# Batch 0's v loaded by key block for six heads, and the first transposes of batch 1 one column block sooner

## The chip, the cores and the metric

The kernel runs on one core of one Trainium2 chip. The metric is the device time of one launch in microseconds (us), the median of several runs. One further execution was taken with the hardware profiler; all times of single instructions below are from it, counted from its first instruction.

The engines have short names in the profile: PE is TensorE (matrix products and transposes), DVE is VectorE, ACT is ScalarE, POOL is GpSimd, SP is SyncE. Each runs its own list of instructions in order and waits on semaphores for the others. Loads and stores (DMAs) are issued by SP, ACT or POOL and then run by themselves.

## The reference

A decayed causal attention over 8 batches of 8 heads, followed by a two-layer network with an exact GELU. Cut to what is computed:

```python
# q, k, v: (8, 8, 576, 64)   f: (8, 8, 576)   w_in: (512, 2048)   w_out: (2048, 512)
scores = q @ k.T / sqrt(64)
cum    = cumsum(log(clip(f, 1e-4, 1)))
scores = where(causal, scores + cum[i] - cum[j], -1e9)
attn   = softmax(scores)
x      = (attn @ v).transpose(0, 2, 1, 3).reshape(8 * 576, 512)
out    = gelu(x @ w_in) @ w_out
```

## The kernel before

**Stages.** Each batch has an attention stage, four pairs of heads at a time, and then gemm1 (x @ w_in with GELU) by column blocks of 128 of the 2048 hidden columns. gemm2 (g @ w_out) of a batch is spread into the attention of the next one. The order on every engine is the order in which the program issues it; nothing is reordered by a scheduler. Batch 0 has its own `first_attention`, batch 1 its own `second_attention`, batches 2 to 7 share `attention`. The last 64 rows of all batches go through one more gemm1 and gemm2 at the end.

**v and the decay.** The decay is folded into v: `weigh_v(b, i)` (L288) multiplies v of pair i with a weight per key into the bf16 tile `vw`, with one more column that gives the softmax's denominator. The tile `v_sb` has the shape [128 keys, 8 heads, 5 key blocks, 64]. For batch 0 blocks 0 to 3 are filled by a loop over the heads on POOL's queue (L168 to L172), one load of 128 KB per head; block 4 has a load of its own later (`load_v` with block 4, L134). The helper `load_v(b, h0, h1, eng, ns)` loads v by key block instead: one load per block n for the heads h0 to h1.

**Where v of batch 0 is used.** In `first_attention` DVE does `weigh_v` of pairs 0 and 1, POOL that of pairs 2 and 3. Ahead of the latter POOL issues block 0 of w_in, block 4 of v and block 1 of w_in (`load_w_in` L184). The POOL queue has at most eight loads under way: a load waits for the landing of the eighth before it.

**The chain of batch 0's attention.** `scores_0` (L619) writes the scores of 128 keys against a range of queries, with the causal mask added by PE; ACT takes the exponential (L624). `attend_0(i, h)` (L650) multiplies the exponentials with `vw` into a PSUM bank `o`; the pool `o_psum` has two banks, in turn. `divide` (L663 reciprocal, L664 product) reads the bank, so that attend_0(1, 0) waits for the division of (0, 0), and so on. `to_xT_0` (L674) transposes the result on PE, and a copy (L677) puts it where gemm1 reads it.

**q and k.** In batches 0 and 1 they are transposed on PE: `transposes_first(b, i, ...)` (L226) makes 36 transposes of 64x64 for pair i into two banks of `o_psum`, and DVE copies them to `qT[i]` and `kT[i]` (L241). The q and k rows of heads 0 to 3 of batch 1 come with two loads that POOL issues in `first_attention`.

**gemm1 of batch 0.** `gemm1(c, ffb)` (L405) takes four matmuls of 128x512 for column block ffb and then a gelu on ACT (L425). Column blocks 0 to 3 are in `first_attention`, 4 to 9 in the loop at the end of the kernel, and 10 to 15 are held back for `second_attention`. The loop hangs other work behind some column blocks:

```python
                if ffb == 7:
                    weigh_v(1, 0)
                    load_w_out(0)
                    weigh_v(1, 1)
                    load_w_out(1)
                    load_qk_tokens(2)
                if ffb == 8:
                    transposes_first(1, 0, o_psum, "o")
```

`second_attention` begins with a switch of ACT's table to the exponential (L894) and with `scores` (L319) of pair 0, two tiles; then come the transposes of pair 1, two held column blocks and the next two tiles of scores. The scores' pool `s_psum` has two buffers, and ACT's exponentials (L329) free them.

Of the kernel before, what the change touches and what calls it, by code (L numbers as in the profile page):

```python
# [18 lines left out]
H = 8  # L19
HP = 4  # L20
NBLK = 5
# [33 lines left out]
def kernel(  # L55
# [10 lines left out]
    nc = tc.nc  # L66
# [31 lines left out]
    def load_qk_tokens(b, h0=0, h1=H):  # L98

        if b >= B:  # L100
            return
        stacked = b < 2
        if b not in qk_of:
            qk_of[b] = [
                qk_pool.tile(
                    [P, H // 2, J0 * D] if stacked else [PT, H, JT * D],
                    BF16,
                    tag=n,
                    name=f"{n}{b}",
                )  # L110
                for n in "qk"
            ]
        for which, src in enumerate((q, k)):
            if stacked:
                half, g0 = divmod(h0, H // 2)
                g1 = h1 - half * (H // 2)
                dst = qk_of[b][half][which * D : (which + 1) * D, g0:g1, :]
            else:
                dst = qk_of[b][which][:, h0:h1, :]
            nc.gpsimd.dma_start(  # L120
                dst,
                src[b, h0:h1].rearrange(
                    "h (p j) d -> p h (j d)", j=J0 if stacked else JT
                ),
            )
# [3 lines left out]
    def load_v(b, h0=0, h1=H, eng=nc.sync, ns=range(NBLK)):  # L129
        if b >= B:  # L130
            return
        for n in ns:
            p0 = D if n == NBLK - 1 else 0
            eng.dma_start(  # L134
                v_sb[p0:P, h0:h1, n, :],
                v[b, h0:h1, K0[n] + p0 : K0[n] + P].rearrange("h p d -> p h d"),
            )
# [27 lines left out]
    load_qk_tokens(0, 4, 6)  # L165
    diagonal(after, Alu.is_ge, -1.0e9, D)
    load_qk_tokens(0, 6, 8)
    for h in range(H):  # L168
        nc.gpsimd.dma_start(
            v_sb[:, h, 0 : NBLK - 1, :],  # L170
            v[0, h, 0:TC].rearrange("(n p) d -> p n d", p=P),
        )  # L172

    qT = [consts.tile([P, S], BF16, name=f"qT{i}") for i in range(HP)]
    kT = [consts.tile([P, S], BF16, name=f"kT{i}") for i in range(HP)]
# [10 lines left out]
    def load_w_out(c):  # L186
        kt = slice(c * n_ff // 4, (c + 1) * n_ff // 4)
        nc.gpsimd.dma_start(w_out_sb[:, kt, :], w_out_r[:, kt, :])
# [94 lines left out]
    def weigh_v(b, i, eng=nc.gpsimd, n0=0, n1=NBLK):  # L283

        hs = slice(2 * i, 2 * i + 2)
        bh = b * H + 2 * i
        w = wT[:, n0:n1, bh : bh + 2].rearrange("p n h -> p h n")
        eng.tensor_tensor(  # L288
            vw(b)[:, hs, n0:n1, 0:D],
            v_sb[:, hs, n0:n1, :],  # L290
            w.unsqueeze(3).to_broadcast([P, 2, n1 - n0, D]),
            Alu.mult,
        )
        if b:
            eng.tensor_copy(vw(b)[:, hs, :, D], w)
# [104 lines left out]
    def gemm1(c, ffb, kts=range(4), ps=None, act=True):  # L400
        src = xT(c) if c < B else tails
        if ps is None:
            ps = m_psum.tile([P, TC], FP32, tag="m", name="ps1")
        for kt in kts:
            nc.tensor.matmul(  # L405
                ps,
                w_in_sb[:, kt, ffb * P : (ffb + 1) * P],
                src[:, kt, 0:TC],
                start=(kt == 0),
                stop=(kt == n_dm - 1),  # L410
            )
        if n_dm - 1 in kts and act:
            gelu(c, ffb, ps)
        return ps

    def spare():
        return o_psum.tile([P, TC], FP32, tag="o", name="ps1")

    def gelu(c, ffb, ps):
        if c not in g_of:  # L420
            g_of[c] = [
                g_pool.tile([P, TC], BF16, tag=f"g{n}", name=f"g{n}")
                for n in range(n_ff)
            ]
        nc.scalar.activation(g_of[c][ffb], ps, Act.Gelu)  # L425
# [253 lines left out]
    def attend_tail():  # L679
        o = o_psum.tile([P, NBLK, D + 1], FP32, tag="o", name="o")  # L680
        for i in range(HP):
            for n in range(NBLK):
                e, c = e0_of[i, n, True]
                for h in range(2):
                    nc.tensor.matmul(
                        o[h * D : (h + 1) * D, i, :],
                        e[:, h, c + TC : c + S],
                        vw_of[0][:, 2 * i + h, n, :],
                        start=(n == 0),
                        stop=(n == NBLK - 1),  # L690
                    )
        x = x_pool.tile([P, NBLK, 2, D], BF16, tag="x", name="x")
        x_of[0, "tail"] = x.rearrange("p n h d -> p (n h) d")[:, 0:HP]
        divide(x_of[0, "tail"], o, HP)

    def tail_0():
        ps = o_psum.tile([P, HP, TL], BF16, tag="o", name="ps_x")
        for i in range(HP):
            for h in range(2):
                d = slice(h * D, (h + 1) * D)  # L700
                nc.tensor.transpose(
                    ps[d, i, :], x_of[0, "tail"][d, i, :], ident_bf[d, d]
                )
        nc.vector.tensor_copy(tails[:, :, 0:TL], ps)
# [176 lines left out]
    def second_attention():  # L881


        b, fill = 1, gemm2_first(0)

        def av(i, h):
            attend(b, i, h, (0, 1, 2, 3, 4))
            normalize(b, i, h)

        def transposes(i, pool, tag):  # L890
            transposes_first(b, i, pool, tag)


        nc.scalar.activation(warm[0:1, 0:1], warm[0:1, 0:1], Act.Exp)  # L894
        def tiles(i, t):
            scores(b, i, t)
            scores(b, i, t + 1)

        def run(i):
            av(i, 0)  # L900
            av(i, 1)

        tiles(0, 0)
        transposes(1, o_psum, "o")
        gemm1_hold(10)
        gemm1_hold(11)
        tiles(0, 2)
        gemm1_hold(12, nc.scalar.copy)
        transposes(2, o_psum, "o")
        tiles(1, 0)  # L910
        gemm1_hold(13)
        run(0)
        tiles(1, 2)
        gemm1_hold(14, nc.scalar.copy)
        transposes(3, o_psum, "o")
        weigh_v(1, 2)
        tiles(2, 0)
        gemm1_hold(15)
        run(1)
        weigh_v(1, 3)  # L920
        tiles(2, 2)
        take(fill, 4)
        tiles(3, 0)
        transpose_dma(2, 0, 4)
        transpose_dma(2, 4, 8)
        to_xT(b, 0, nc.vector.tensor_copy, o_psum, "o")
        to_xT(b, 1, nc.vector.tensor_copy, o_psum, "o")
        take(fill, 4)
        tiles(3, 2)
        behind(qk_of[2][1], H - 1)  # L930
        load_w_out(2)
        load_w_out(3)
        run(2)
        take(fill, 4)
        av(3, 0)
        take(fill, 4)
        both = s_psum.tile([P, 2, 1024], BF16, tag="s", name="ps_x2")
        to_xT(b, 2, nc.scalar.copy, ps=both[:, 0, 0:XC])
        av(3, 1)
        gemm1_begin(1, both)  # L940
        x_tail(1)
        load_v(2)

    for b in range(B):
        if b == 0:
            first_attention()
        elif b == 1:
            second_attention()
        else:
            attention(b)  # L950
        for ffb in range(4 if b < 2 else 5, n_ff):
            if b == 0 and ffb in HELD:
                continue
            aside = ffb in (7, 8) if b > 1 else b == 1 and ffb % 4 < 2
            gemm1(b, ffb, ps=spare() if aside else None)
            if b == 1 and ffb % 2 == 0:
                at = HELD[(ffb - 4) // 2]
                gelu(0, at, h_of[at])
            if b == 0:
                if ffb == 4:  # L960
                    attend_tail()
                if ffb == 5:
                    tail_0()
# [3 lines that stand above are left out]
                    weigh_v(1, 1)  # L967
                    load_w_out(1)
                    load_qk_tokens(2)
                if ffb == 8:  # L970
                    transposes_first(1, 0, o_psum, "o")
            elif b + 1 < B:
                first, gap = (5, 3) if b == 1 else (1, 4)
                at, late = divmod(ffb - first, gap)
                if late == 0:
                    untangle(b + 1, at)
                if late == gap - 2 and (b > 1 or at < 2):
                    weigh_v(b + 1, at)
                if ffb == (9 if b == 1 else 14):
                    load_qk_tokens(b + 2)  # L980
# [34 lines left out]
```

## Time and profile before

| | |
|---|---|
| three runs | 336.19, 333.74, 334.04 us |
| median | 334.04 us |
| the profiled execution | 335.58 us |
| its span, first to last instruction | 333.8 us |
| PE busy | 325.1 us (97%) |
| ACT, DVE, POOL busy | 205.5, 184.2, 134.2 us |
| PE's granted clock | 1.000 |

Busy times are sums over the span; the engines overlap. A DMA's landing is the time at which its data have arrived. A line such as `13.68 1.08 issue` of the chain has the start, the length, and the engine with its line; "issue" is time in which the engine waited for nothing that the profile shows. In a timeline a row has start, length, engine, line, operation, what is written from what, the count, and in brackets the idle time before it and what ended that.

### The profile page before, as it was taken

What the parts mean: (1) busy time and instruction counts of PE and PEld (TensorE: products, weight loads), DVE (VectorE), ACT (ScalarE), POOL (GpSimd) and SP (SyncE); (2) the same over time, 40 slices, a digit from 0 to 9 for tenths busy, and PEclk for the clock granted to TensorE, in tenths of its full rate; (3) what the DMA queues carried; (4) which work ended last, traced back from release to release, by engine and by line L of the source; (5) the groups of instructions that cost most, each with busy time, mean ns of one, the idle gap of its engine ahead of it and who ended that gap; (6) DMA issues with size and microseconds to landing.
All of it is one profiled execution on the core that took longest, in us unless ns stands there. A gap on an engine that the chain in (4) does not pass through costs nothing.

```text
span 333.8 us, 8055 instructions
## 1 busy us (share of the span) xinstructions
PE 325.1 (97%) x3287; PEld 170.1 (51%) x3287; DVE 184.2 (55%) x427; ACT 205.5 (62%) x296; POOL 134.2 (40%) x260
## 2 busy tenths in 40 slices
PE   8899999999999999999999999999999999999995
PEld 4664555445554466445644565455544654444443
DVE  5852657474549855894589547954795450010011
ACT  4786886974535786478736892788278836405600
POOL 8897873039327054704472354534442420000000
PEclk9999999999999999999999999999999999999999
DMA  7899999989999899389939895889700420021022
GB/s 118 192 202 218 206 194 98 195 170 156 206 195 179 133 219 157 92 136 175 209 111 141 160 174 157 115 153 212 155 1 3 100 75 33 0 89 38 0 50 77
DMA packets 94948, 44.18 MB, mean 132 GB/s; under 512 B 74176, under 2 KB 89792, under 8 KB 94912
## 3 DMA queue, kind: packets, MB, share of 16 engines
q1 hardware_dynamic: 77760, 27.16, 42.6%
q0 software_dynamic: 16752, 15.99, 30.7%
q8 instruction: 25, 0.41, 0.5%
q10 hardware_dynamic: 400, 0.52, 0.4%
q14 instruction: 11, 0.09, 0.1%
HBM read 36.85 MB, written 9.44 MB: 139 GB/s over the span
## 4 chain that ended last, share of the span: by engine, by line
PE 95%; ACT 2%; DVE 1%; issue 1%; DVEq 0%
PE ps L405 37%; PE ps L509 27%; PE ps L449 8%; PE o L350 8%; PE s L319 7%; PE s L619 1%; PE ps_w L210 1%; PE ps_f L226 1%; ACT e L624 1%; PE ps L569 1%; PE ps L545 1%; PE o L650 0%; ACT e L329 0%; PE ps_x L383 0%; DVE x L664 0%
## 5 line engine op out<-in xcount | busy, mean ns | idle before, releaser
L425 ACT ACTIVATE g<-ps 128x512 bf16<-128x512 f32 x138 | 78.5, 602 | 79.5 <-PE ps L405 78.9
L405 PE MATMUL ps<-xT,w_in_sb 128*128 128x512 bf16 x512 | 114.1, 379 | 0.1
L509 PE MATMUL ps<-w_out_sb,g 64*128 64x512 bf16 (+1 forms) x711 | 108.5, 377 | 0.0
L329 ACT ACTIVATE e<-s 128x896 bf16<-128x896 f32 x112 | 87.7, 836 | 21.3 <-PE s L319 18.8
L405 PEld LDWEIGHTS <-w_in_sb 128*128 128x128 bf16 x576 | 55.3, 98 | 66.6 <-issue 2.6
L331 POOL TENSOR_SCALAR_AFFINE_SELECT e<-e 128x256 bf16<-128x256 bf16 (+1 forms) x135 | 49.1, 383 | 87.5 <-ACT e L329 87.1
L509 PEld LDWEIGHTS <-g 64*128 64x128 bf16 (+1 forms) x711 | 40.2, 95 | 34.8 <-issue 4.7
L288 POOL TENSOR_TENSOR vw<-v_sb,wT 128x640 bf16<-128x640 f32 (+1 forms) x30 | 38.3, 1278 | 26.1 <-PE s L319 16.2
L269 DVE COPY kT<-tk 64x288 bf16<-64x288 bf16 x96 | 46.1, 480 | 1.6
L269 DVE COPY qT<-tq 64x288 bf16<-64x288 bf16 x96 | 36.7, 383 | 5.8 <-DMA tq<-q 4.4
L517 DVE COPY ot<-ps 128x512 f32<-128x512 f32 x20 | 13.8, 691 | 47.2 <-PE ps L509 47.2
L319 PE MATMUL s<-qT,kT 64*128 64x256 bf16 (+2 forms) x336 | 37.6, 276 | 0.8 <-DVE kT L241 0.6
L350 PEld LDWEIGHTS <-e 128*128 128x128 bf16 x840 | 30.3, 98 | 7.9 <-POOL e L331 2.5
L458 DVE COPY ot<-ps 128x512 f32<-128x512 f32 (+2 forms) x9 | 5.7, 632 | 49.6 <-PE ps L449 49.6
L350 PE MATMUL o<-vw,e 128*128 128x65 bf16 x840 | 32.3, 194 | 0.0
L364 DVE TENSOR_TENSOR x<-o,r 128x320 bf16<-128x320 f32 x56 | 27.5, 492 | 3.2 <-DMA xT<-x 1.3
L449 PE MATMUL ps<-w_out_sb,g 128*128 128x512 bf16 (+2 forms) x144 | 28.0, 355 | 0.0
L319 PEld LDWEIGHTS <-kT 64*128 64x128 bf16 x336 | 16.9, 94 | 19.2 <-issue 4.2
L449 PEld LDWEIGHTS <-g 128*128 128x128 bf16 x144 | 13.5, 98 | 14.5
L529 DVE TENSOR_TENSOR ot<-ot,ps 128x512 f32<-128x512 f32 x22 | 15.1, 685 | 1.1
L363 DVE RECIPROCAL r<-o 128x5 f32<-128x5 f32 x56 | 10.5, 187 | 9.1 <-PE o L350 9.1
L405 PE MATMUL ps<-tails,w_in_sb 128*128 128x512 bf16 x64 | 14.3, 377 | 0.0
(89 smaller groups left out, 186.8 us busy)
## 6 DMA issues: line engine op xcount, KB each, us to landing
out_dram<-ot SPq DMA_DIRECT2D x32, 256.0 KB, 2.4
v_sb<-in_v_dram SPq DMA_DIRECT2D x24, 256.0 KB, 5.1
q<-in_q_dram POOLq DMA_DIRECT2D x6, 576.0 KB, 6.6
k<-in_k_dram POOLq DMA_DIRECT2D x6, 576.0 KB, 8.6
v_sb<-in_v_dram POOLq DMA_DIRECT2D x17, 128.0 KB, 6.5
w_in_sb<-in_moe_w_in_dram POOLq DMA_DIRECT2D x4, 512.0 KB, 7.2
w_out_sb<-in_moe_w_out_dram POOLq DMA_DIRECT2D x4, 512.0 KB, 9.4
v_sb<-in_v_dram SPq DMA_DIRECT2D x6, 128.0 KB, 4.6
```

The costliest lines, as they stand in the source:

```text
L269: nc.vector.tensor_copy(rows[:, odd], src[odd * D : (odd + 1) * D, 2 * i + h].rearrange("d j p -> d p j"),)
L288: eng.tensor_tensor(vw(b)[:, hs, n0:n1, 0:D], v_sb[:, hs, n0:n1, :], w.unsqueeze(3).to_broadcast([P, 2, n1 - n0, D]), Alu.mult,)
L319: nc.tensor.matmul(to, *ab, start=half < 0, stop=half == 1 or not masked)
L329: nc.scalar.activation(et[:, :, z:c], st[:, :, z:c], Act.Exp, scale=scale)
L331: nc.gpsimd.affine_select(out=et[:, :, c0 + z : c0 + P], in_=et[:, :, c0 + z : c0 + P], compare_op=Alu.is_ge, fill=0.0, base=z, pattern=[[ ...
L350: nc.tensor.matmul(o[:, m, :], e_of[b, i, t][:, h, c : c + P], vw_of[b][:, 2 * i + h, n, :], start=(n == 0), stop=(n == m),)
L364: nc.vector.tensor_tensor(x_of[b, i][:, :, h, :], o[:, :, 0:D], r.unsqueeze(2).to_broadcast([P, NBLK, D]), Alu.mult,)
L405: nc.tensor.matmul(ps, w_in_sb[:, kt, ffb * P : (ffb + 1) * P], src[:, kt, 0:TC], start=(kt == 0), stop=(kt == n_dm - 1),)
L425: nc.scalar.activation(g_of[c][ffb], ps, Act.Gelu)
L449: nc.tensor.matmul(pss[ts][:, c0:c1], g_of[c][kt][:, ts * P : (ts + 1) * P], w_out_sb[:, kt, c0:c1], start=(kt == 0), stop=(kt == n_ff - 1),)
L509: nc.tensor.matmul(banks[r], g_of[c][kt][rows, ts * P : (ts + 1) * P], w_out_sb[rows, kt, :], start=kt == (steps.index("r") if r else 0), ...
L529: nc.vector.tensor_tensor(ot, ot, bank, Alu.add)
```

## The change

In the set-up, the loop over the heads loads heads 0 and 1 only. Heads 2 to 7 are loaded by `load_v`, one load for each of the key blocks 0 to 3, all six heads in it (192 KB). In the loop at the end, the transposes of batch 1's first pair are issued behind column block 7, after the loads that POOL issues there, instead of behind column block 8.

```diff
-    for h in range(H):
+    for h in range(2):
         nc.gpsimd.dma_start(
             v_sb[:, h, 0 : NBLK - 1, :],
             v[0, h, 0:TC].rearrange("(n p) d -> p n d", p=P),
         )
+    load_v(0, 2, H, nc.gpsimd, range(NBLK - 1))
...
                     weigh_v(1, 1)
                     load_w_out(1)
                     load_qk_tokens(2)
-                if ffb == 8:
+                if ffb == 7:
                     transposes_first(1, 0, o_psum, "o")
```

The function that is called in place of the loop:

```python
    def load_v(b, h0=0, h1=H, eng=nc.sync, ns=range(NBLK)):
        if b >= B:
            return
        for n in ns:
            p0 = D if n == NBLK - 1 else 0
            eng.dma_start(
                v_sb[p0:P, h0:h1, n, :],
                v[b, h0:h1, K0[n] + p0 : K0[n] + P].rearrange("h p d -> p h d"),
            )
```

## The prediction

> **What bounds the kernel now.** I read the page first, then the chain of work that ended last in two windows, then the engines' timelines there and the landings of the loads.
>
> ```profile
> PE 325.1 (97%) x3287; PEld 170.1 (51%) x3287; DVE 184.2 (55%) x427; ACT 205.5 (62%) x296; POOL 134.2 (40%) x260
> ...
> PE 95%; ACT 2%; DVE 1%; issue 1%; DVEq 0%
> ```
>
> TensorE (PE) is busy for 97% of the span and is 95% of the chain. So only a change of PE's waits can move the end, and a wait that PE gains or loses early on is carried to the end: from 22.33 us on the chain is PE work with few breaks. The two edits touch two such places. The first is batch 0's attention. These are rows of the chain from 12 to 23 us (start, length, what):
>
> ```profile
> 13.68 1.08 issue
> 14.76 0.28 PE s L619 x4
> ...
> 17.05 0.56 PE s L619 x12
> 17.61 0.44 PE o L650 x10
> 18.05 0.02 issue
> 18.07 0.19 DVE r L663
> 18.27 0.02 issue
> 18.29 0.42 DVE x L664
> ```
>
> Here PE and VectorE (DVE) hand work to each other: attend_0 (L650) writes an `o` bank, the division (L663, L664) frees it, and there are two banks. DVE's own timeline shows what stands ahead of those divisions:
>
> ```profile
> 14.74 1.48 DVE L288 TENSOR_TENSOR vw<-v_sb,wT 128x512 bf16<-128x512 f32 x2 [0.99 <-DMA v_sb<-in_v_dram]
> 16.13 0.18 DVE L663 RECIPROCAL r<-o 128x4 f32<-128x4 f32 x1
> 16.34 0.42 DVE L664 TENSOR_TENSOR x<-o,r 128x256 bf16<-128x256 f32 x1
> ```
>
> The two multiplications are weigh_v of pairs 0 and 1, and the first division follows them without a pause. Thus a late v of heads 2 and 3 delays every division.
>
> The second place is the start of batch 1, in the chain from 31 to 38 us and on ScalarE (ACT):
>
> ```profile
> 31.74 0.48 PE ps_f L226 x36
> ...
> 32.32 0.62 issue
> 32.94 0.76 DVE kT L241
> ...
> 33.74 0.73 PE s L319 x18
> ```
>
> ```profile
> 33.77 1.28 ACT L894 ACT_TABLE_LOAD   x1
> 35.06 0.20 ACT L894 ACTIVATE warm<-warm 1x1 bf16<-1x1 bf16 x1
> 35.17 1.58 ACT L329 ACTIVATE e<-s 128x896 bf16<-128x896 f32 x2
> 37.13 1.51 ACT L329 ACTIVATE e<-s 128x896 bf16<-128x896 f32 x2 [0.38 <-PE s L319]
> ```
>
> PE stands still before 33.74 until kT is copied, and right behind it ACT loads a table and cannot start its exponentials before 35.17.
>
> **Edit 1, the loads: issue.** Six loads of one head each (128 KB) become four of 192 KB; bytes (0.75 MB) and runs of 256 B stay. GpSimd (POOL) takes 0.75 to 0.83 us for a v load of 512 runs. A load of 768 runs is not among the v loads; the nearest row is a q load of [8,96] runs with 0.79, and in proportion to the runs it would be 1.5 x 0.75 = 1.13. I take 0.79 because that row has the same count. The four then start at 8.61, 9.40, 10.19 and 10.98, against the last head load at 12.68 before. By either price POOL is done sooner, by 1.6 us or by 0.3 us.
>
> **Edit 1: landing.** Issue does not set the landing. The trace's semaphore counts give one step per queue ring, sixteen per load. For the last head load fifteen rings are done at 15.52 and the last one at 16.87. Last counts of heads 0 to 7: 12.79, 14.64, 15.11, 15.43, 15.73, 16.10, 16.49, 16.87. Two views agree with that:
>
> ```profile
> L288 POOLq EVENT_SEMAPHORE  x2: 17/30/42, 16.1 to 16.9; - x2
> ```
>
> ```profile
> DMA to landing us min/median/max: 4.2/4.8/5.7
> ```
>
> The first (the multiplications' line, 10 to 20 us) has POOL's semaphore waits ahead of weigh_v of pairs 2 and 3, the last of them at 16.9. The second (the tile v_sb, 12 to 18 us) has as its minimum the load issued at 12.68, which gives 16.88. The late ring always has work queued (head 0 was issued at 7.09 and leaves it at 12.79), so issuing sooner cannot help it. It moves the same twelve packets of 4 KB for heads 2 to 7 at 0.195 us each, in another order. I therefore put the last block's landing at 16.87, where the last head landed.
>
> Pair 1 needed heads 2 and 3 only (15.43); now it needs all four blocks. Its multiplication starts 0.08 after the landing (15.52 after 15.44 before), so at 16.95 instead of 15.52: **1.43 us late**.
>
> The Trainium skill, DMA: Bandwidth & Descriptors, section Anatomy of one DMA, speaks otherwise: a load takes about 2.0 us and its bytes at 436 GB/s. By that estimate a block of 196,608 bytes takes 2.45 us and lands before 13.5, and edit 1 would cost nothing. The head loads here took 4.2 to 6.8 us, so I go by the rows.
>
> Why is that ring late? In the second from 12 to 13 us the DMA view shows one 16 KB packet of the instruction queue; it starts at 12.27 and takes 1.23. PE's unexplained 1.08 us ends at 14.76, next to head 1's last count. I infer that an instruction fetch sat on this ring. PE's program up to there is not changed, so I expect it again. The Trainium skill, Runtime: NRT & Kernel Launch, section Instruction fetch mechanics, calls the cost of such a refill mostly hidden. If it were, the last count would come with the other fifteen, at about 15.52, and edit 1 would again cost nothing.
>
> **Edit 1: who waits.** The multiplication takes 0.69 and ends at 17.64. Behind it in DVE's queue are the divisions of pair 0. Before, they ended 0.55 and 1.10 after the multiplication's end (16.76 and 17.31 after 16.21), so now at 18.19 and 18.74. PE's attend_0(1,0) reuses the bank of (0,0); from the end of a division to the matmul the trace has 0.15 (18.71 to 18.86). So it starts at 18.34 rather than 17.54, and attend_0(1,1) at 18.89. Its ten matmuls take 0.44, then come four transposes, 0.38, so attend_0(2,0) starts at 19.71. It started at 18.86: **0.85 us late**. Of the 1.43 us, 0.58 go into waits that PE had there anyway. Everything after is handed on in the same order, so 0.85 reaches 22.33 and with it the end. Edit 1 costs nothing if the last block lands by 15.43 + 0.58 = 16.01, and one for one beyond.
>
> POOL's weigh_v of pair 2 starts at 16.95 instead of 16.39 and ends at 18.03; pair 3 ends at 19.1. PE wants them at 19.71 and past 21.5, so that is hidden by edit 1's own delay. Behind them w_in block 2 and q, k of batch 1 are issued 0.6 later, while w_in blocks 0 and 1 (1 MB, to 22.87 before) keep the rings full. In return POOL issues w_in block 0 up to 1.6 us sooner, into a lull: 73 GB/s from 15 to 16 us. This makes later loads land somewhat sooner and nobody on the chain waits for them: w_in 0 is first read at 21.64 and was there at 19.57.
>
> **Edit 2, the transposes.** 36 transposes (0.41 us of PE's time) go ahead of column block 8 instead of behind it; no work is added. They would start at 31.67 - 0.86 = 30.81. Their q tile has landed by 28.75, and DVE reads their two banks for the last time at 28.09 and 29.09. Behind them in DVE's queue only batch 1's copies come. qT and kT are then ready 0.86 sooner, at 32.83. PE leaves column block 9 at 32.94 (32.08 and four matmuls at 0.216, from the chain's 12.95 us for 60 of them). So nothing is left of the wait ahead of 33.74: 33.74 - 32.94 = 0.80 us.
>
> But little of it is kept. Column block 9's gelu still starts at 33.15, so ACT's table load and the first exponential stay at 35.17. The tile pool of scores has two buffers. The fourth scores tile needs the second exponential's end, 36.75, and started at 36.93: with 0.04 for the release (47.12 to 47.16 in the chain) PE gains 36.93 - 36.75 - 0.04 = **0.14 us** there, and waits the rest. From 37.31 to 45.26 the chain is PE, so 0.14 is what it keeps. Bounds: 0, if the release is slower, and 0.80, if ACT did not bind. I take 0.14, because both rows are read at the very place. The same holds when edit 1 shifts PE and ACT alike.
>
> **The sum.** 0.85 - 0.14 = +0.71 us. The profiled execution took 335.58 (span 333.8 and 1.78 around it), so 336.29 by its own time. It lies 1.54 above the median of the runs, 334.04; the same difference put on the median gives **334.8**.
>
> **Rivals.** (A) *The late ring is not late*: without the hold the last count comes at about 15.52, before 16.01. Edit 1 is free and 0.14 is gained: 333.9. For it: fifteen of sixteen rings; against it: the late ring is the last one for every v load of batch 0. (B) *ACT does not bind*: edit 2 keeps its whole 0.80, and 0.85 - 0.80 = +0.05: 334.1. Against it: the exponentials stand back to back from 35.17. (C) *Slower*: the late ring runs at the pace of batch 1's v loads, whose last counts lie 0.59 to 0.69 apart per 128 KB (29.10, 29.69, 30.38, 31.00), since w_in now follows the v loads without the lull. Six times 0.63 from 14.64 gives 18.4; that is 2.97 late, less 0.58, less 0.14: +2.25, so 336.3. It costs from a landing of 16.01 on, and would reach 1% at 19.5. Against it: 0.195 per packet held at 16.0 to 16.5, with w_in already flowing. (D) *PE's clock falls in the longer pauses*: the nine warm-up matmuls took 0.447 each against 0.216 later, over 4.8 us until the full clock is recorded at 6.07; half of that is 2.4, with edit 1's shift 337.1. Against it: the pause of 1.08 us at 13.68 left the clock at 1.00, and the new one is about as long.
>
> **How the numbers follow.** The forecast has 0.50, A 0.20, B 0.10, C 0.15, D 0.05. The range reaches from A with the most that edit 2 can give (-0.80), 333.2, to a little over C, 336.5; D is left out. About 1% is what a measurement of this kernel can tell from no change: 330.7 to 337.4. No case gives a gain of 3.3 us, so faster gets 0.02 for what no row shows; slower gets 0.05, from D and the far end of C; within 1% 0.93.
>
> **What would show it.** Right: DVE's second multiplication near 16.95, waiting for v; attend_0(2,0) about 0.85 later; no wait of PE on kT at batch 1's start, and in its place a wait on the exponential ahead of the fourth scores tile. Wrong: pair 1 weighed before 16.0 (then A), after 18 (then C), a clock under 1.00 near 18 us (D), or batch 1's fourth scores tile moved by less than 0.3 (B).

## The result, and the profile after

The changed kernel has a median of 335.42 us over 22 runs, the kernel before 334.40 in the same session: a ratio of 1.0029, 95% interval 1.0015 to 1.0042, or +0.97 us (0.5 to 1.4). So it is a little slower, by less than 1%. The ratios here, and the counts by clock further down, leave out executions that the chip disturbed. The two profiled executions stand the other way round, 335.58 before and 335.18 after (spans 333.8 and 333.2): each is one execution, and that of before was an unusually long one, as the runs below show.

The page of the changed kernel, busy time and shares of the chain:

```profile
PE 320.7 (96%) x3244; PEld 169.6 (51%) x3287; DVE 184.1 (55%) x427; ACT 205.8 (62%) x296; POOL 133.5 (40%) x258
PE 90%; POOL 4%; issue 2%; DMA 2%; ACT 1%; DVE 0%; POOLq 0%; ACTq 0%
```

PE is still nearly the whole chain, but DMA and POOL are new on it. (43 of its 3287 matmuls are missing from this trace, so its busy time is not to be compared.) The chain from 8 to 24 us shows where they come in (start, length, what):

```profile
8.75 2.38 POOL v_sb L134 x3
11.13 5.35 DMA v_sb<-in_v_dram
...
16.64 2.60 POOL vw L289 x2
19.24 0.46 PE o L651 x10
```

The block load issued last, at 11.13, takes 5.35 us, lands at 16.48, and everything behind it follows. What DVE and PE do with it, in their timelines:

```profile
14.03 0.69 DVE L289 TENSOR_TENSOR vw<-v_sb,wT 128x512 bf16<-128x512 f32 x1 [0.28 <-DMA v_sb<-in_v_dram]
16.60 0.69 DVE L289 TENSOR_TENSOR vw<-v_sb,wT 128x512 bf16<-128x512 f32 x1 [1.88 <-DMA v_sb<-in_v_dram]
17.21 0.18 DVE L664 RECIPROCAL r<-o 128x4 f32<-128x4 f32 x1
...
18.65 0.42 DVE L665 TENSOR_TENSOR x<-o,r 128x256 bf16<-128x256 f32 x1
```

```profile
17.90 1.03 PE L651 MATMUL o<-vw,e 128*128 128x65 bf16 x20 [1.13 <-DVE x L665]
...
19.22 0.47 PE L651 MATMUL o<-vw,e 128*128 128x65 bf16 x10
...
33.17 0.28 PE L320 MATMUL s<-qT,kT 64*128 64x256 bf16 x2
...
36.92 0.31 PE L320 MATMUL s<-qT,kT 64*128 64x320 bf16 x2 [0.24 <-ACT e L330]
```

Pair 0 is weighed at once, pair 1 stands 1.88 us for its v, and the divisions behind it make PE wait 1.13 us. The chain puts attend_0(2,0), at 19.22, down to POOL. But it joins POOL's two multiplications (2.60 us, to 19.24) in one row, and pair 2 is the first of them. The division shown last ends at 19.07, and 0.15 from a division to the matmul is what the prediction had read; so I take DVE as what releases it.

At the start of batch 1 (33.17) PE no longer waits for kT. It waits 0.24 us for an exponential ahead of the fourth scores tile instead, because ACT's side has not moved: its table load stands 14.67 us behind attend_0(2,0) here and 14.68 in the second profile of before (e7, below).

```profile
33.89 1.28 ACT L895 ACT_TABLE_LOAD   x1
...
35.29 2.96 ACT L330 ACTIVATE e<-s 128x896 bf16<-128x896 f32 x4
```

### The profile page after: what moved, and what is told of

The parts are those of the page before. It is cut to its first block, busy times and chain, and to the rows that moved or that the text cites. A ratio compares the mean times of both kernels' runs of the same rounds, so it can differ in the third digit from the quotient of the medians.

```text
span 333.2 us, 8009 instructions
## 1 busy us (share of the span) xinstructions
PE 320.7 (96%) x3244; PEld 169.6 (51%) x3287; DVE 184.1 (55%) x427; ACT 205.8 (62%) x296; POOL 133.5 (40%) x258
## 4 chain that ended last, share of the span: by engine, by line
PE 90%; POOL 4%; issue 2%; DMA 2%; ACT 1%; DVE 0%; POOLq 0%; ACTq 0%
PE ps L406 37%; PE ps L510 26%; PE o L351 8%; PE ps L450 8%; PE s L320 6%; DMA v_sb<-in_v_dram 2%; PE ps L570 1%; ACT e L330 1%; POOL vw L289 1%; PE ps L546 1%; POOL v_sb L134 1%; POOL k L120 1%; POOL q L120 1%; POOL v_sb L169 0%; PE ps_x L384 0%
## 5 line engine op out<-in xcount | busy, mean ns | idle before, releaser
L406 PE MATMUL ps<-xT,w_in_sb 128*128 128x512 bf16 x494 | 112.7, 379 | 1.3 <-DVE xT L678 0.3
L510 PE MATMUL ps<-w_out_sb,g 64*128 64x512 bf16 (+1 forms) x692 | 104.4, 376 | 1.6 <-issue 1.3
L510 PEld LDWEIGHTS <-g 64*128 64x128 bf16 (+1 forms) x711 | 39.4, 95 | 34.7 <-issue 4.2
L270 DVE COPY kT<-tk 64x288 bf16<-64x288 bf16 x96 | 42.8, 446 | 3.3 <-DMA tk<-k 1.8
L270 DVE COPY qT<-tq 64x288 bf16<-64x288 bf16 x96 | 39.9, 416 | 3.1 <-DMA tq<-q 1.7
L320 PE MATMUL s<-qT,kT 64*128 64x256 bf16 (+1 forms) x336 | 37.1, 276 | 0.5 <-ACT e L330 0.4
```

The lines of the kernel that those rows point to most:

```text
L270: nc.vector.tensor_copy(rows[:, odd], src[odd * D : (odd + 1) * D, 2 * i + h].rearrange("d j p -> d p j"),)
L320: nc.tensor.matmul(to, *ab, start=half < 0, stop=half == 1 or not masked)
L406: nc.tensor.matmul(ps, w_in_sb[:, kt, ffb * P : (ffb + 1) * P], src[:, kt, 0:TC], start=(kt == 0), stop=(kt == n_dm - 1),)
L510: nc.tensor.matmul(banks[r], g_of[c][kt][rows, ts * P : (ts + 1) * P], w_out_sb[rows, kt, :], start=kt == (steps.index("r") if r else 0), ...
```

## Experiments

The theory: edit 1 makes pair 1 wait for the last of four blocks (+0.85), edit 2 gives only 0.14 because ACT binds. The main rivals: the loads cost nothing; edit 2 keeps its whole 0.80; the longer pause halves PE's clock.

**The two kernels again.** e7_before_again is the kernel before, e8_after_again the changed one, both unchanged.

> The kernel before once more, to have a second profile of it. In the first profile PE stood 1.08 us at 13.68 with no wait that shows, and span 333.8 lies at the upper end of the runs of before. Theory: that pause is not in the usual execution; without it the first multiplication starts near 14.0 and the second near 14.7, when head 3 has landed, the fourth scores tile of batch 1 starts 0.9 to 1.5 us sooner than 36.93, and the span is 332.0 to 332.8. Rival (the pause is usual and the first profile stands for the runs): the pause of about 1 us is there again, and the second multiplication starts near 15.5.

> The changed kernel once more, for a second profile and on the same chip as the one before. Theory: the second multiplication starts at 16.4 to 17.0 whatever PE did before, attend_0(1,0) waits for it 1 us or more, and the time is 0.7 to 1.4 us over before; the span is 333.0 to 334.3, the upper end where the clock is at half for one stretch of 3.4 us behind that wait. Rival (the time was lost elsewhere): the multiplication starts before 16.0, or the time is within 0.3 us of before.

Measured: 334.37 us, 0.9991 (0.9971 to 1.0011), and 335.64 us, 1.0034 (1.0012 to 1.0055). The first one's DVE and PE timelines, then the second one's:

```profile
14.65 0.69 DVE L288 TENSOR_TENSOR vw<-v_sb,wT 128x512 bf16<-128x512 f32 x1 [0.30 <-DMA v_sb<-in_v_dram]
```

```profile
17.62 0.48 PE L650 MATMUL o<-vw,e 128*128 128x65 bf16 x10 [0.29 <-POOL vw L288]
...
35.46 0.30 PE L319 MATMUL s<-qT,kT 64*128 64x320 bf16 x2
...
36.74 0.72 PE L226 MATMUL ps_f<-key_of,k 64*64 64x64 bf16 x36
```

```profile
16.29 0.69 DVE L289 TENSOR_TENSOR vw<-v_sb,wT 128x512 bf16<-128x512 f32 x1 [1.75 <-DMA v_sb<-in_v_dram]
```

```profile
38.68 0.47 PE L227 MATMUL ps_f<-key_of,k 64*64 64x64 bf16 x34 [0.56 <-DMA k<-in_k_dram]
```

In this execution of before pair 1 is weighed at 14.65 and attend_0(2,0) starts at 17.62, not 15.52 and 18.86 as in the first profile. The pause of 1.08 us without a cause shown is missing: PE has 0.25 at 13.21 in its place. That is what was expected of e7; e8 came out as expected too, but for the second multiplication, which starts just under the 16.4 named. Over the profiles at full clock in which heads 0 to 7 are loaded one by one, attend_0(2,0) starts at 17.61 to 18.05 in four (e7, e9, e10, e11 below) and at 18.86 in the first profile; with both edits it starts at 19.22 and 18.91. So against those four edit 1 costs 0.9 to 1.6 there, 1.6 between e7 and the profile after; against the first profile it would be only 0.05 to 0.36. At the fourth scores tile e7 and the profile after are 1.46 apart (36.92 against 35.46): edit 2 gives back 0.14. Counted from attend_0(2,0), that tile starts 17.70 or 17.71 later in four profiles with edit 2 (after, e8, e3, e10) and 17.83 or 17.84 later in e7 and e9 (18.07 in the first profile). At the end e7 and the profile after are 1.2 apart, which is 1.60 less 0.14 and less the 0.24 by which the k tile holds up e7 (next paragraph); the medians of the time differ by less, since this execution of before (span 332.0) lies at the short end of its runs, whose spans have a median of about 332.6.

The lower lines show a wait that I had not foreseen: the k tile of heads 4 to 7. It holds up the transposes of pair 2, which read it, in e7 (0.72 instead of 0.48; its last count is at 36.95) and by 0.56 in e8 (38.64), but not in the first profile after (36.53). It comes and goes, and blurs the comparison by about half a microsecond.

**Each edit alone.** e1_blocks_only has edit 1, e2_transposes_only edit 2:

```diff
-    for h in range(H):
+    for h in range(2):
...
+    load_v(0, 2, H, nc.gpsimd, range(NBLK - 1))
```

```diff
-                if ffb == 8:
+                if ffb == 7:
```

> Edit 1 alone: heads 2 to 7 by key block, the transposes where they were. Theory (the last ring's landing delays DVE's second multiplication): that multiplication starts between 16.4 and 17.0 us instead of 15.52, attend_0(2,0) is 0.4 to 0.9 late, and the time is 0.5 to 1.6 us over before, about 1.1, which is what the whole change cost (0.97 by the ratio) plus the 0.14 that edit 2 gave. Rival 1 (the loads cost nothing and the moved transposes cost it): no difference from before, within 0.3. Rival 2 (the clock falls in the longer pause): over 2.5 us, with a granted clock under 1.00 near 18 us.

> Edit 2 alone: the loads as before, the transposes one column block sooner. Theory (ACT's table load and exponentials bind right behind): PE's first scores of batch 1 start 0.8 us sooner, its fourth scores tile only 0.1 to 0.2 sooner behind a wait on an exponential, and the time is 0 to 0.3 us under before, about 0.14. Rival 1 (ACT does not bind): 0.8 us under before. Rival 2 (the move is what cost the time): about 1 us over before.

Measured: 336.82 us, 1.0083 (1.0052 to 1.0114, 6 runs), and 335.12 us, 1.0017 (0.9996 to 1.0039, 12 runs). The first, +2.8 us, is above the 0.5 to 1.6 expected and where Rival 2 put it; the second decides nothing, for its interval holds no change. The profile of edit 2 alone, in windows (window, length, busy time of PE, PEld, DVE, ACT and POOL, PE's clock, DMA share, GB/s), is no help either: the clock was halved in a stretch where the kernel is still the same as before.

```profile
10.70:17.60 6.90, 6.90 (x119) 4.60 (x114) 5.40 (x8) 5.14 (x6) 6.67 (x9) 0.51 1.00 193
```

So I ran edit 1 alone again, in 12 runs (e12_blocks_again, the same code as e1_blocks_only).

> Edit 1 alone once more. Its first six runs gave 0.83% over before, 2.8 us, where the second profile of before against that of the change puts edit 1 at 1.6 us (attend_0(1,0) at 17.9 instead of 16.3) and edit 2 at 0.35 against it. Theory (1.6 us by the late landing; more only where the clock is at half for 3.4 us, or comes up late at the start, as in two of those six): 1.2 to 2.0 us over before, a span of 333.4 to 334.2 in the usual execution and some 0.5 to 1.3 more with half a clock behind the pause. Rival (edit 2 hides more than half of edit 1's cost): 2.4 us or more over before again, in executions at full clock too.

Measured: 336.26 us, 1.0044 (1.0005 to 1.0083), or +1.5 us: within the 1.2 to 2.0 expected, but with an interval of 0.2 to 2.8. Windows of its profile:

```profile
16.00:19.60 3.60, 1.89 (x45) 1.47 (x41) 2.83 (x9) 2.15 (x3) 2.96 (x3) 0.95 1.22 223
19.60:23.10 3.50, 3.50 (x77) 3.32 (x75) 1.76 (x8) 2.41 (x4) 3.21 (x6) 0.56 0.92 143
```

In the first window PE is busy for 1.89 of 3.60 us, and in the next it runs at about half clock. The profile of e1_blocks_only has the same. DVE's multiplication (16.59) and attend_0(1,0) (17.89) stand where they stand in the profile after; only then do they part, and at 25 us they are 1.1 us apart. Five of these 12 executions have a mean clock of 0.992 or 0.993 and spans of 333.9 to 334.5; those at 0.997 and above have 332.9 to 333.5, but for one; the other two, at 0.977 and 0.985, have 336.8. So rival D is real in part of the executions. A mean clock under 0.996 is found in 8 of 17 executions of edit 1 alone, in 5 of 34 with both edits, and in 3 of 92 of the kernel before. Why edit 2, which comes later, should lower that share isn't explained, and stays open.

**More blocks.** e5_all_blocks loads all eight heads by block, without edit 2, so that pair 0 waits too:

```diff
-    for h in range(H):
...
+    load_v(0, 0, H, nc.gpsimd, range(NBLK - 1))
```

> All eight heads by key block (four loads of 256 KB), the transposes where they were: the suspected wait made larger, since pair 0 now waits for the last block too. Theory: the first multiplication starts at 16.4 to 17.0 instead of near 14.0, attend_0(0,0) 2 to 2.8 us late, and the time is 2.0 to 3.5 us over before. Rival (PE has other work there, or a later wait takes the delay up): under 1.2 us over before.

Measured: 338.05 us, 1.0092 (1.0058 to 1.0126), +3.1 us. DVE and PE:

```profile
17.14 2.16 DVE L284 TENSOR_TENSOR vw<-v_sb,wT 128x512 bf16<-128x512 f32 x2 [3.64 <-DMA v_sb<-in_v_dram]
```

```profile
17.88 1.16 PE L646 MATMUL o<-vw,e 128*128 128x65 bf16 x20 [2.51 <-DVE vw L284]
```

The wait moves to the first multiplication (17.14, a little past the 16.4 to 17.0 expected) and grows, as the theory has it. All six executions have mean clocks of 0.989 to 0.995; the profile has half clock for 3.41 us from 18.04 on, so part of the 3.1 us is the clock's.

**Fewer blocks.** e3_pair1_by_head loads heads 0 to 3 by head and only 4 to 7 by block, with edit 2; e6_pair1_no_move does the same without edit 2.

```diff
-    for h in range(H):
+    for h in range(4):
...
+    load_v(0, 4, H, nc.gpsimd, range(NBLK - 1))
```

> Both edits, but heads 0 to 3 are loaded by head and only heads 4 to 7 by key block (four loads of 128 KB), so DVE's pair 1 waits for head 3 alone while pairs 2 and 3, on POOL, wait for the last block. Theory (only pair 1's wait costs): the second multiplication starts near 15.5 again and the time is that of edit 2 alone, 0 to 0.3 us under before. Rival (the order by block costs through POOL's later multiplications or through the loads behind them): it stays about 1 us over before.

> Only heads 4 to 7 by key block, heads 0 to 3 by head, the transposes where they were. It parts the two readings of the run with both (0.33% over before, while pair 1 was on time again). Theory (only pair 1's wait costs): the second multiplication starts near 14.5 and the time is that of before within 0.4 us. Rival (the blocks of heads 4 to 7 cost by themselves, through POOL's pairs 2 and 3 or the loads behind): 0.6 to 1.2 us over before, and the profile shows PE waiting for pair 2, pair 3 or a later load.

Measured: 335.01 us, 1.0033 (1.0000 to 1.0066), and 335.09 us, 1.0016 (0.9984 to 1.0048). The profile of e3_pair1_by_head, DVE and then PE:

```profile
14.53 0.69 DVE L289 TENSOR_TENSOR vw<-v_sb,wT 128x512 bf16<-128x512 f32 x1 [0.18 <-DMA v_sb<-in_v_dram]
```

```profile
17.61 0.48 PE L651 MATMUL o<-vw,e 128*128 128x65 bf16 x10 [0.29 <-DVE r L664]
...
37.33 0.47 PE L227 MATMUL ps_f<-key_of,k 64*64 64x64 bf16 x34 [0.50 <-DMA k<-in_k_dram]
```

With heads 2 and 3 back in loads of their own, pair 1 is on time and attend_0(2,0) starts at 17.61 as in e7: the delay in batch 0 comes from pair 1's dependence on the last block. The time missed its expectation: it did not fall to that of before. At +1.1 us, with an interval of 0 to 2.2, it stands where the Rival put it, so the runs' times do not confirm that pair 1's wait is the whole of the +0.97 us. The profiled execution itself ends only 0.4 us behind e7 (span 332.4 against 332.0). In it POOL's multiplications wait for the last block (16.09 against 15.53 in e7), the loads behind them are issued 0.56 later, and PE waits 0.50 for the k tile. e6_pair1_no_move is inconclusive: its interval reaches into both readings, and its profile ran at half clock until 20.44 us. What blocks for heads 4 to 7 cost by themselves stays open.

**Is it ACT that keeps edit 2's gain?** e4_hold9 has edit 2 and column block 9 held back for batch 1, so that ACT's table load comes one gelu sooner:

```diff
-    HELD = range(10, 16)
+    HELD = range(9, 16)
...
-                if ffb == 8:
+                if ffb == 7:
...
+        gemm1_hold(9)
```

> Edit 2 alone with column block 9 of batch 0 added to the held ones: its four matmuls stay in their place, but DVE copies the result and its gelu runs in batch 1's column blocks, so ACT's table load for the exponential follows column block 8. Theory (ACT binds behind edit 2): the table load starts about 0.8 us sooner, the fourth scores tile starts 0.5 to 0.8 us sooner than before without a long wait on an exponential, and the time is 0.4 to 0.8 us under before. Rival (something else than ACT takes edit 2's gain, such as PE's own order or DVE's copies): the time is that of edit 2 alone, 0 to 0.3 us under before, or above it by the extra copy.

Measured: 334.54 us, 1.0015 (0.9997 to 1.0033): no gain, a miss. Its profile started at half clock and cannot be read for times. Because the k tile might have taken the gain, three more kernels load it sooner: e9_k_sooner is the kernel before with this order, e10_k_sooner_move adds edit 2, e11_k_sooner_hold9 adds column block 9 held as well.

```diff
+        load_qk_tokens(1, 4, 8)
+        load_w_in(3)
...
-        load_w_in(3)
-        load_qk_tokens(1, 4, 8)
```

> Before, with one thing moved: q and k of batch 1's heads 4 to 7 and w_in block 3 are issued behind q and k of heads 0 to 3, ahead of batch 1's v. A control for the next two. Theory (that k tile's landing, 36.95 to 38.64 us in the profiles, stands just behind PE's transposes of pair 2 in the usual execution of before): the tile lands before 34, PE loses no wait or 0.1 to 0.3 us of it, and the time is 0 to 0.4 us under before. Rival (no part in it): no difference within 0.2 us.

> The same order of loads with edit 2. Edit 2 alone and the run with pair 1 by head gained nothing; the profile of the latter has a wait of 0.50 us for the k tile ahead of the transposes of pair 2. Theory (the landing of the k tile took what edit 2 had gained): without that wait the time is 0.2 to 0.6 us under before, and the rest of edit 2's gain still goes to ACT's exponentials (0.24 us of wait at the fourth scores tile). Rival (edit 2's gain is lost elsewhere): no difference from before, or over it as with edit 2 alone (0.17%).

> The same order of loads with edit 2 and column block 9 held, so that neither ACT's table load nor the k tile's landing is behind edit 2. Theory (these two are what edit 2 runs into): PE starts the fourth scores tile without a wait and goes on without one at the transposes of pair 2; the time is 0.5 to 1.0 us under before. Rival (only one of them binds, or the held block's copy and later gelu cost as much): 0 to 0.3 us under before.

Measured: 338.71 us, 1.0130 (1.0097 to 1.0163); 337.72 us, 1.0092 (1.0066 to 1.0118); 337.53 us, 1.0108 (1.0090 to 1.0127). PE in the second and the third:

```profile
35.31 0.31 PE L319 MATMUL s<-qT,kT 64*128 64x320 bf16 x2 [0.24 <-ACT e L329]
...
36.61 0.48 PE L226 MATMUL ps_f<-key_of,k 64*64 64x64 bf16 x36
```

```profile
34.85 0.30 PE L319 MATMUL s<-qT,kT 64*128 64x320 bf16 x2
```

e10 and e7 reach attend_0(2,0) at the same time (17.61 and 17.62), so their rows can be set side by side. The fourth scores tile is 0.15 sooner with edit 2 (35.31 against 35.46), behind the same wait of 0.24 for the exponential, and the k tile holds up nothing. With the table load sooner (e11) that wait is gone and the tile comes another 0.46 sooner, although its attend_0(2,0) was 0.10 later. So it is ACT that keeps the rest of edit 2's gain. All three lose more than that later: they are 3.1 to 4.3 us over before, where a gain was expected. POOL's waits in e9_k_sooner between 20 and 60 us (line, what for, us in total, times, longest):

```profile
POOL v_sb L134 <- DMA w_in_sb<-in_moe_w_in_dram: 3.8, 2, 1.9
```

Behind w_in block 3, POOL's loads of v wait for a landing of w_in before they can be issued, and POOL's other work waits behind them: in e10 PE waits 0.71 ahead of 44.46 for POOL's work on the exponentials (L331). In e9 it also waits 1.67 ahead of 73.87 in gemm2, for a copy on DVE; whether that goes back to POOL isn't shown, nor do these waits add up to the whole loss. No other kernel tried here was faster than the kernel before.

## Why the prediction was right, point by point

Forecast 334.8 and no change beyond 1%; measured +0.97 us where the sum gave +0.71.

- **Which wait.** Right: pair 1's multiplication waits for the last block, the divisions follow it, and PE loses time at attend_0(1,0). The profiles of e3_pair1_by_head (one dependence taken away) and e5_all_blocks (one added) show it; the time of e3 leaves open how much of the +0.97 comes from it.
- **The last block's landing.** Forecast 16.87, measured 16.48 and in e8 16.16. The late ring was there, as said (15 of 16 are done by 15.83), but 0.65 behind the others rather than 1.35, and 0.28 in e8. Issuing POOL's loads sooner did not help, as said: the last block was issued at 11.13 and landed at 16.48, where in e7 the last head was issued at 12.47 and landed at 16.01. The Trainium skill, DMA: Bandwidth & Descriptors, section Anatomy of one DMA, gives an estimate of 2.45 us for a block; this trace has 5.35 for the last, issued with earlier loads still under way, and the measurement decides.
- **1.43 late, 0.58 of slack, 0.85 on the path: the term that was mis-sized.** Against e7 the multiplication is 1.95 late (16.60 against 14.65), PE takes up 0.35 of it, and 1.60 are left; over the profiles, the first one left out, the term is 0.9 to 1.6. The step that failed is its base. I took an execution with an unusual pause of 1.08 us as the rule and wrote "I expect it again". It isn't in e7, where head 3 lands at 14.56 rather than 15.43, and that pause had delayed before's own path and so hidden a part of what edit 1 costs. The two errors, a base too late and a landing too late, partly cancelled; that +0.71 comes so near +0.97 is in part luck. Such a pause stands once more in e5_all_blocks (1.05 us, up to 14.48), and in these two profiles the packet of the instruction queue starts late: at 12.09 (not 12.27, as I had read) and 11.83, against 10.1 to 11.1 in the nine others that are at full clock there. That fits an instruction fetch behind the pause, but no run shows it. The Trainium skill, Runtime: NRT & Kernel Launch, section Instruction fetch mechanics, calls the refill mostly hidden: e7 agrees (0.25 of pause); the first profile (1.08) does not, if its pause is such a refill.
- **Edit 2 keeps 0.14.** Right at its place: 0.14 between e7 and the profile after (1.60 less 1.46), 0.15 in e10. ACT is the reason (e11). By the time alone the gain cannot be told from nothing, with or without edit 1.
- **Not foreseen:** the k tile's wait of 0 to 0.56 us at pair 2's transposes. I had written that nobody on the chain waits for the loads issued behind; e3 and e8 show that PE does.
- **The rivals.** A fell: the multiplication starts at 16.29 to 16.60 in all four profiles with edit 1, not near 15.5. B fell: the wait went over to ACT. C fell: with edit 1 no block of heads 2 to 7 landed after 16.5. D I had argued away too easily. From "the pause of 1.08 left the clock at 1.00" I concluded that one about as long would; the pauses with edit 1 were 1.04 to 1.59, and the longer ones were followed by half clock. It is in part of the executions, and its price is 1.1 us (e12 against the profile after, at 25 us) rather than 2.4, so D belongs in the upper end of the range and not outside it.

## What to carry to other kernels

A load that is split by what its consumer needs first is not the same as one split into equal pieces of the whole: before merging loads, ask which consumer now waits for the last piece, and on which queue that consumer stands ahead of others. Before a sum is built on a row of one profile, ask whether the row belongs to the program or to that execution: an unexplained "issue" of a microsecond on the path is reason for two values of the base, not one. And work moved sooner gains only up to the next thing that binds, here ACT's table and exponentials, then a transfer.

## What the runs showed of the hardware

Half clock behind short pauses. PE's clock fell to 0.5 for 3.41 us from 19.61, behind a pause of 1.39 at 17.89 (e1_blocks_only); from 19.27 behind one of 1.59 (e12_blocks_again); from 18.04 behind 2.51 (e5_all_blocks). Pauses of 1.13 and 1.04 at the same place (the two profiles with both edits), and that of 1.08 at 13.68 in the first profile, left it whole. Where the pause falls may count as well as its length. In the clock's records every stretch but the cut-off last one lasts a whole multiple of 3.413 us (13.65, 6.83, 3.41, 310.61), and in the 3.41 us that end with each of these three falls PE was busy for 1.91, 1.70 and 0.90 us. The 3.41 us of the same grid that hold the pauses without a fall have 2.16 (after), 2.37 (e8) and 2.33 (first profile). But in e2_transposes_only the clock fell at 10.76, for 6.83 us, behind 3.41 us with 2.60 of work and no pause over 0.63, and e9_k_sooner kept the full clock behind as little (6.03 to 9.45). So what decides is not shown. The Trainium skill, TensorE: Matmul & The Clock Gate, section HAM oscillation — how this bites in real kernels, gives pauses over about 3.4 us as what to avoid; here far shorter ones were followed by half clock.
